# A routed expert layer's narrow last tiles: second product with the weights stationary, turned back at the end of the unit

## The chip, the core and the metric

The kernel runs on one core of one Trainium2 chip. The metric is the device time of one execution in microseconds (us); lower is better. Before the change three runs took 534.16, 530.08 and 535.13 us, median 534.16.

## What is computed

A block-sparse attention (4 batches, 8 heads, 768 positions, head size 64) gives 3072 tokens of 512 numbers. These go through a mixture of 8 experts: every token is sent to the one expert with the largest gate logit and multiplied by that token's two gates.

```
x = attention(q, k, v, sampled_blocks)          # [3072, 512]
e_idx = argmax(x @ w_gate)                       # one expert of 8 for each token
for e in range(8):
    mask = e_idx == e
    h  = maximum(x[mask] @ w1[e], 0)             # 512 -> 1024, first product
    ye = h @ w2[e]                               # 1024 -> 512, second product
    out[mask] = gate_w[mask] * eom[mask, e] * ye
```

Only the second product `h @ w2[e]` of some tokens, and the way to the output of those tokens, is touched by the change.

## The kernel before

**Stages.** The attention takes the first half of the span. From about 262 us on the kernel works through the experts in units. A unit is one expert's weights and up to three tiles of tokens. `SHAPE` (line 50) lists the tiles of each unit by their number of tokens: unit 0 to unit 13 run here, and the eight units behind them (`rest`, line 1302) stand under a branch on the number of tokens and are not entered in this input. Six of the fourteen units end in a tile of less than 128 tokens: unit 2 is [128, 128, 96], unit 4 [128, 128, 32], unit 10 [32], unit 11 [128, 64], unit 12 [128, 32], unit 13 [32]. All others are [128, 128].

**Steps.** Each unit has eight chunks of 128 hidden numbers (`NFC`), so there are 112 chunks, and one step of the program handles one chunk number n. `program` (line 1191) puts the functions of a step in order of a rank, and the engines carry them out in that order: the order on every engine is fixed (`in_order`). In step n stand: `w_h` and `w_l` of chunk n+6 (ScalarE and VectorE split the 32-bit weights into two 16-bit halves), `p_h` of chunk n (TensorE, first product, line 991), `p_y` of chunk n-4 (TensorE, second product, line 1031, since `YL` is 4), then `h_h` and `h_l` (ScalarE and VectorE split the hidden numbers into two 16-bit halves `hh`, `hl`). A unit u ends with its last `p_y` in step 8u+11. In step 8u+12 `y_o` (line 1059) scales the result by the gate on ScalarE and moves it from PSUM to SBUF, and a step later `store_y` (line 1067) writes the rows to their places with an indirect DMA of GpSimd.

**First product.** `p_h` keeps the weights stationary, 128x128 at a time, and moves the unit's tokens past them: 12 matmuls a chunk, as many columns as the unit has tokens.

**Second product.** `p_y` keeps the hidden numbers of a tile of t tokens stationary (128 by t) and moves 512 columns of w2 past them: three matmuls a chunk for a tile of 128 or 96 (hh with both halves of the weights, hl with one). For a tile of 32 or 64 tokens it cuts the 512 columns into 4 or 2 parts and writes them to different partitions of PSUM, so that each matmul uses 32 or 64 columns of the array: 12 matmuls of 128 columns, or 6 of 256. The result then lies as [128, 128] or [128, 256], and the table of output rows is made to fit this by three extra GpSimd instructions in `keep_t` (lines 880 to 886, with the constant `cb` of line 303).

**Buffers around it.** The hidden numbers come from two PSUM banks (`psT`, tag T). The results y stand in `psS` for units of more than one tile (the third tile, and the only tile of a unit of one, in `psO`, which has two banks). Converted weights go round a ring of 12 places, so `w_h` of chunk n waits for `p_y` of chunk n-12.

Of the kernel before, what the change touches and what calls it, by code (L numbers as in the profile page):

```python
# [9 lines left out]
F32 = mybir.dt.float32  # L10
F16 = mybir.dt.float16
I32 = mybir.dt.int32
AF = mybir.ActivationFunctionType
ALU = mybir.AluOpType
# [6 lines left out]
DM = H * D  # L21
E, FF = 8, 1024
NTOK = B * S
# [5 lines left out]
XP = DM + 16  # L29
# [20 lines left out]
SHAPE = [[128, 128]] + [widths(CAPS[w - NPU] if NPU <= w < NPU + NR else 8) for w in WALK]  # L50
# [10 lines left out]
YL = 4  # L61
# [65 lines left out]
def tile_kernel(ctx, tc, q, k, v, sampled, wg, wcat, out):  # L127
    nc = tc.nc
# [37 lines left out]
    ea = const.tile([128, 4], F32, name="ea")  # L166
    eai = const.tile([1, 1], I32, name="eai")
    xs0 = const.tile([128, 1024], F32, name="xs0")
    cb = const.tile([128, 2], F32, name="cb")
    rowid = const.tile([128, PS, MT], F32, name="rowid")  # L170
    arow = const.tile([128, 2], F32, name="arow")
    place_u = const.tile([128, 1 + PS, MT], I32, name="place_u")
# [119 lines left out]
    def setup_index():  # L292
        pp = psO.tile([128, 512], F32, tag="O", name="pp")
        for m in range(5):
            nc.tensor.matmul(pp[0:PS, m:m + 1], pw[:, :, m], ones[0:1, 0:1], start=True, stop=True)
        nc.vector.tensor_copy(index, pp[0:PS, 0:5])

        vf = sp.tile([128, 2, 12], F32, name="vf")
        nc.vector.tensor_copy(vf, vi)
        nc.vector.tensor_single_scalar(pb[:, 2:3], pb[:, 0:1], 63, op=ALU.bitwise_and)  # L300
        nc.vector.tensor_single_scalar(pb[:, 0:1], pb[:, 0:1], 6, op=ALU.arith_shift_right)
        nc.vector.tensor_single_scalar(pb[:, 1:2], pb[:, 1:2], 5, op=ALU.arith_shift_right)
        nc.vector.tensor_copy(cb, pb[:, 0:2])
        nc.vector.tensor_single_scalar(pb[:, 1:2], pb[:, 1:2], 1, op=ALU.bitwise_and)
        pf = sp.tile([128, 4], F32, name="pf")
        nc.vector.tensor_copy(pf[:, 0:2], pb[:, 0:2])
        nc.vector.tensor_copy(pf[:, 3:4], pb[:, 2:3])
        for w in range(NPU, NPU + NR):
            sh = widths(CAPS[w - NPU])
            if sh[-1] in (32, 64):  # L310
                m = len(sh) - 1
                nc.vector.tensor_single_scalar(
                    rowid[:, w, m:m + 1], rf if sh[-1] == 32 else pf[:, 3:4], 128.0 * m, op=ALU.add)

        nc.vector.scalar_tensor_tensor(pf[:, 2:3], pf[:, 0:1], 768.0, rf, op0=ALU.mult, op1=ALU.add)
        nc.vector.scalar_tensor_tensor(pf[:, 3:4], pf[:, 1:2], 736.0, pf[:, 2:3], op0=ALU.mult, op1=ALU.add)
        nc.vector.scalar_tensor_tensor(pf[:, 2:3], pf[:, 1:2], 32.0, pf[:, 2:3], op0=ALU.mult, op1=ALU.add)
        nc.vector.tensor_scalar(vf[:, :, 1:12], vf[:, :, 1:12], pf[:, 2:3], -32.0, op0=ALU.add, op1=ALU.add)
        nc.vector.tensor_scalar(vf[:, :, 0:1], vf[:, :, 0:1], pf[:, 3:4], None, op0=ALU.add)
        nc.vector.tensor_copy(vals, vf.rearrange("p a b -> p (a b)"))  # L320
# [532 lines left out]
    def piece(s, j):  # L853
        return rbuf[(8 * s + j) % NRAW]

    regs, tabs, xfs, xgs, xs, ws, hps, hs, ys, yos = {}, {}, {}, {}, {}, {}, {}, {}, {}, {}
    NP = NUNIT * NFC
    toks = [sum(sh) for sh in SHAPE]
    per = [2 if t <= 256 else 1 for t in toks]
# [8 lines left out]
    def keep_t(u):  # L868
        sh = SHAPE[u]
        m = len(sh)  # L870
        tab = rt.tile([128, MT], I32, tag="tab", name=f"tab{u}", bufs=4)
        gate = rt.tile([128, MT], F32, tag="gate", name=f"gate{u}", bufs=4)
        tabs[u] = tab, gate
        if not u:
            for n, x in enumerate(xfs[u]):
                nc.gpsimd.tensor_copy(gate[:, n:n + 1], x[:, DM + 1:DM + 2])
                nc.gpsimd.tensor_copy(tab[:, n:n + 1], x[:, DM:DM + 1])
            return
        nc.gpsimd.tensor_copy(gate[:, 0:m], xfs[u][:, :, DM + 1])
        if sh[-1] in (32, 64):  # L880
            m -= 1
            f = rt.tile([128, 1], F32, tag="tabf", name=f"tabf{u}")
            nc.gpsimd.tensor_single_scalar(f, xfs[u][:, m, DM:DM + 1], 128.0 / sh[-1], op=ALU.mult)
            c = 1 if sh[-1] == 32 else 0
            nc.gpsimd.tensor_tensor(f, f, cb[:, c:c + 1], op=ALU.add)
            nc.gpsimd.tensor_copy(tab[:, m:m + 1], f)
        if m:
            nc.gpsimd.tensor_copy(tab[:, 0:m], xfs[u][:, 0:m, DM])

    def load_w(n):  # L890
        if n in (0, 2, 8):
# [139 lines left out]
    def p_y(n):  # L1031
        u = n // 8
        hh, hl = hs[bank_of(n)]
        sh = SHAPE[u]
        if n % 8 == 0:
            y = ys[u] = []
            if u and len(sh) > 1:
                t = psS.tile([128, 2, 512], F32, tag="S", name=f"y{u}")
                y.extend((t[:, 0], t[:, 1]))
            while len(y) < len(sh):  # L1040
                y.append(psO.tile([128, 512], F32, tag="O", name=f"y{u}_{len(y)}"))
        k = cols(n).start
        if not u:
            for m in range(2):
                nc.tensor.matmul(  # L1045
                    ys[0][m], hh[:, k + 128 * m:k + 128 * m + 128], piece(0, n)[:, 512:1024], start=n == 0, stop=n == 7)
            return
        w = ws.pop(n)
        for t, y in zip(sh, ys[u]):
            parts = 128 // t if t in (32, 64) else 1  # L1050
            d = DM // parts
            for cnt, (a, l) in enumerate(((hh, 0), (hh, 1), (hl, 0))):
                for p in range(parts):
                    nc.tensor.matmul(  # L1054
                        y[t * p:t * p + t, 0:d], a[:, k:k + t], w[:, l, 512 + d * p:512 + d * p + d],
                        start=n % 8 == 0 and cnt == 0, stop=n % 8 == 7 and cnt == 2)
            k += t

    def y_o(u):
        yos[u] = []  # L1060
        for m, (w, y) in enumerate(zip(SHAPE[u], ys.pop(u))):
            rows_, d = (128, DM * w // 128) if w in (32, 64) else (w, DM)
            t = att.tile([128, XP], F32, tag="P", name=f"yo{u}_{m}", bufs=6)[0:rows_, 0:d]
            nc.scalar.activation(t, y[0:rows_, 0:d], AF.Copy, scale=tabs[u][1][0:rows_, m:m + 1])  # L1064
            yos[u].append(t)

    def store_y(u):
        tab = tabs.pop(u)[0]
        for m, (w, t) in enumerate(zip(SHAPE[u], yos.pop(u))):
            rows_, d = t.shape  # L1070
            c = DM // d
            i = nc.gpsimd.indirect_dma_start(  # L1072
                out.rearrange("n (c d) -> (n c) d", c=c), bass.IndirectOffsetOnAxis(ap=tab[0:rows_, m:m + 1], axis=0), t, None,
                bounds_check=NTOK * c - 1, oob_is_err=False).ins

            tc.declare_no_dep(i, group="out", reason="rows of out differ")
            tc.add_to_no_dep_group("out", i)
# [113 lines left out]
    def program(n0, n1):  # L1191
# [11 lines left out]
        for u in range(NUNIT):  # L1203
# [4 lines left out]
                do(max(t - 8, WW), 13, x_s, u)  # L1208
            do(max(t - 6, WW if u else 0), 13, keep_t, u)
            do(XT.get(u, max(t - 6, WW)), 15, x_t, u)  # L1210
            do(t + 8 + YL, 12, y_o, u)
            do(t + 8 + YL + 1, 13, store_y, u)
        for n in range(NP):
            w = max(n - LEAD, WW + (n - 8) // 2)
# [156 lines left out]
```

## Time and profile before

| | |
|---|---|
| runs | 534.16, 530.08, 535.13 us (median 534.16) |
| profiled execution, its time | 531.68 us |
| its span, first to last instruction | 529.9 us |
| TensorE clock granted, mean of the span | 0.982 of full |
| TensorE (PE) busy | 499.7 us, 94% |
| VectorE (DVE) busy | 358.4 us, 68% |
| ScalarE (ACT) busy | 305.8 us, 58% |
| GpSimd (POOL) busy | 256.8 us, 48% |

The span is cut by the profile into groups of instructions by the line that wrote them: L1007 is the first product, L1054 the second product of the units from 1 on, L1064 the scaling `y_o`, L1072 the store, L975 `w_h`, L979 `w_l`, L1021 `h_h`, L1029 `h_l`. The operands are named out<-in; a form 128\*32 128x128 is a stationary operand of 128 by 32 and a moving operand of 128 partitions by 128 columns. Matmuls are pipelined: the time from one start to the next is what a matmul takes from the engine, not the length of its own row. In the chain of waits the pieces follow each other without holes, so a piece's length there is such a distance.

### The profile page before, as it was taken

To read this page: it belongs to the slowest core of one execution; us is meant where nothing else is said; L and a number is where in the kernel's file an instruction comes from. 1 tells how busy PE (TensorE), PEld (TensorE's weight loads), DVE (VectorE), ACT (ScalarE), POOL (GpSimd) and SP (SyncE) were. 2 spreads that over 40 slices of the span, in tenths; PEclk is the share of its full clock that TensorE was granted. 3 is DMA by queue.
4 is the path that set the end of the run, shared out by engine and by line. 5 is a ranking of instruction groups with operands and counts; after the bars stand their busy time and mean duration, and the time that the engine had idled before them with its cause. 6 is when DMAs were issued, how large, how long until landed. Compare 5 with 4: busy or idle time off the path is not lost.

```text
span 529.9 us, 18428 instructions
## 1 busy us (share of the span) xinstructions
PE 499.7 (94%) x7403; PEld 348.9 (66%) x7403; DVE 358.4 (68%) x732; ACT 305.8 (58%) x542; POOL 256.8 (48%) x415
## 2 busy tenths in 40 slices
PE   7989998998988999989999999999999999998994
PEld 6756776766666777768556556666666666666663
DVE  2878879666787697857386545656566666578770
ACT  3646666575554665652376545655556656568661
POOL 7787778680576888854505130422404204126222
PEclk9999999899998999999999999999999999997998
DMA  7967888692976777768899999997998889899901
GB/s 299 300 223 220 259 260 298 216 312 89 274 226 188 240 218 240 243 231 306 295 387 330 409 275 331 354 249 243 260 274 314 250 240 328 233 273 335 220 30 36
DMA packets 63167, 136.60 MB, mean 258 GB/s; under 512 B 30560, under 2 KB 30688, under 8 KB 63074
## 3 DMA queue, kind: packets, MB, share of 16 engines
q1 hardware_dynamic: 50578, 91.56, 56.2%
q0 software_dynamic: 12496, 43.79, 24.7%
q8 instruction: 60, 0.98, 0.8%
q14 instruction: 33, 0.27, 0.1%
HBM read 116.25 MB, written 12.85 MB: 244 GB/s over the span
## 4 chain that ended last, share of the span: by engine, by line
PE 60%; POOL 14%; issue 12%; POOLq 5%; DMA 4%; DVE 4%; ACT 1%; ACTq 0%; DVEq 0%
PE h L1007 23%; PE y L1054 23%; POOL kr L436 7%; POOLq L425 4%; DMA vt<-in_v_dram,vidx 2%; PE S L504 2%; PE T L468 2%; PE h L1000 2%; PE y L1045 2%; POOL rows L757 2%; PE O L547 2%; POOL vt L453 1%; PE O L536 1%; DMA xb<-rows,place_u 1%; DVE mx L511 1%
## 5 line engine op out<-in xcount | busy, mean ns | idle before, releaser
L979 DVE SCALAR_TENSOR_TENSOR kr<-r,kr 128x1024 f16<-128x1024 f32 x77 | 93.8, 1224 | 59.4 <-ACT kr L975 59.0
L1072 POOL DMA_INDIRECT out_dram<-yo,tab x28 | 35.2, 1258 | 178.3 <-ACT yo L1064 174.1
L1007 PE MATMUL h<-xall,kr 128*128 128x256 f16 (+5 forms) x924 | 105.4, 264 | 2.3 <-DVE hh L1029 2.3
L1054 PE MATMUL y<-kr,hh 128*128 128x512 f16 (+3 forms) x675 | 104.3, 316 | 0.0
L975 ACT ACTIVATE kr<-r 128x1024 f16<-128x1024 f32 x77 | 80.8, 1055 | 39.7 <-PE y L1054 34.1
L1007 PEld LDWEIGHTS <-kr 128*128 128x128 f16 x924 | 80.2, 99 | 29.2 <-issue 6.0
L1054 PEld LDWEIGHTS <-hh 128*128 128x128 f16 (+3 forms) x936 | 56.8, 99 | 52.1 <-issue 11.1
L436 POOL TENSOR_TENSOR kr<-kn,eighth 128x256 f32<-128x256 f32 x132 | 79.7, 632 | 7.4 <-issue 5.5
L519 ACT ACTIVATE P<-S,mx 128x256 f32<-128x256 f32 x176 | 69.5, 488 | 9.4 <-DVE mx L511 9.2
L511 DVE TENSOR_REDUCE mx<-S 128x4 f32<-128x1024 f32 x44 | 53.6, 1219 | 21.4 <-ACT P L519 11.5
L453 POOL DMA_INDIRECT vt<-in_v_dram,vidx x44 | 44.4, 1010 | 29.2 <-PE O L547 18.6
L471 ACT COPY pt<-T 128x512 f32<-128x512 f32 x66 | 36.8, 592 | 29.2 <-PE T L468 29.2
L504 PE MATMUL S<-kr,qall 64*32 64x256 f32 x1408 | 50.5, 386 | 2.6 <-POOL kr L436 2.0
L468 PE MATMUL T<-ident,P 128*128 128x128 f32 x352 | 49.1, 284 | 0.0
L1021 ACT ACTIVATE hh<-h 128x512 f16<-128x512 f32 (+5 forms) x60 | 29.0, 484 | 32.2 <-PE y L1054 17.8
L979 DVE SCALAR_TENSOR_TENSOR ws<-r,ws 128x1024 f16<-128x1024 f32 x27 | 33.0, 1223 | 19.0 <-ACT ws L975 18.9
L1029 DVE SCALAR_TENSOR_TENSOR hh<-h,hh 128x512 f16<-128x512 f32 (+5 forms) x60 | 32.8, 546 | 15.3 <-ACT hh L1021 15.3
L468 PEld LDWEIGHTS T<-ident,P 128*128 128x128 f32 x352 | 40.3, 145 | 2.6 <-ACT P L519 0.3
L975 ACT ACTIVATE ws<-r 128x1024 f16<-128x1024 f32 x27 | 28.5, 1057 | 21.5 <-PE y L1054 18.1
L757 POOL DMA_INDIRECT rows<-xall,place x24 | 24.3, 1014 | 27.4 <-DVE dend L480 13.0
L536 PE MATMUL O<-vcall,pt 128*64 128x65 f32 x704 | 31.6, 227 | 5.9 <-DVE pt L473 2.0
L547 PE MATMUL O<-vt,pt 128*32 128x65 f32 x1408 | 31.5, 224 | 4.7 <-DMA vt<-in_v_dram,vidx 4.7
(277 smaller groups left out, 717.4 us busy)
## 6 DMA issues: line engine op xcount, KB each, us to landing
r<-in_wcat_dram SPq DMA_DIRECT2D x112, 512.0 KB, 5.4
vq<-in_v_dram SPq DMA_DIRECT2D x8, 780.0 KB, 5.0
qall<-in_q_dram SPq DMA_DIRECT2D x24, 256.0 KB, 4.5
vcall<-in_v_dram SPq DMA_DIRECT2D x22, 260.0 KB, 4.0
kn<-in_k_dram SPq DMA_DIRECT2D x10, 384.0 KB, 5.4
kn<-in_k_dram SPq DMA_DIRECT2D x3, 768.0 KB, 9.7
vcall<-in_v_dram SPq DMA_DIRECT2D x12, 130.0 KB, 9.4
vt<-in_v_dram,vidx POOLq DMA_INDIRECT x44, 5.3
```

What stands on the lines that cost most here:

```text
L436: nc.gpsimd.tensor_tensor(r[:, slot], kn[bp][:, :, ds(rv, 1)].rearrange("p u o n -> p u (o n)"), e8th, op=ALU.mult)
L453: nc.gpsimd.indirect_dma_start(vt[bp, i][:, s].rearrange("p b j w -> p (b j w)"), None, v, bass.IndirectOffsetOnAxis(ap=vidx[:, bp, i, s:s ...
L468: nc.tensor.transpose(pt[:, 128 * c:128 * c + 128], p[:, 128 * c:128 * c + 128], ident)
L504: nc.tensor.matmul(s[64 * b + 32 * qi:64 * b + 32 * qi + 32, h2, hp], t[p, 64 * j + 32 * qi:64 * j + 32 * qi + 32], g[p, 1 - qi:3:1 + qi, ...
L511: nc.vector.tensor_reduce(mx, self.s.rearrange("p b h n -> p (b h) n"), axis=AX.X, op=ALU.max, negate=True)
L519: nc.scalar.activation(p[:, 256 * hp:256 * hp + 256], self.s[:, b, hp], AF.Exp, bias=self.mx[:, 2 * b + hp:2 * b + hp + 1])
L536: nc.tensor.matmul(o[64 * b:64 * b + 64, h2, hp, 0:VW], t[:, col:col + 64], cv[:, h2, 4 * b + 2 * hg + hp], start=h2 == 0 and hp == 0, sto ...
L547: nc.tensor.matmul(o[row:row + 32, h2, hp, 0:VW], t[:, col:col + 32], av[:, qi, h2, j], start=False, stop=h2 == 1 and hp == 1)
L975: nc.scalar.activation(w[:, 0, r], piece(n // 8, n % 8)[:, r], AF.Copy, scale=SW)
L979: nc.vector.scalar_tensor_tensor(w[:, 1, r], piece(n // 8, n % 8)[:, r], SW, w[:, 0, r], op0=ALU.mult, op1=ALU.subtract)
L1007: nc.tensor.matmul(hps[g][:, cols(n)], w[:, hl, 128 * c:128 * c + 128], x[:, xl, c, 0:t], start=cnt == 0, stop=cnt == 11)
L1054: nc.tensor.matmul(y[t * p:t * p + t, 0:d], a[:, k:k + t], w[:, l, 512 + d * p:512 + d * p + d], start=n % 8 == 0 and cnt == 0, stop=n % 8 ...
```

## The change

For every tile under 128 tokens (so also the one of 96) `p_y` swaps the operands: a 128x128 piece of w2 is stationary, and the t tokens of hh or hl are the moving columns. The result stands turned, as four blocks [128, t] side by side in one PSUM bank, from 12 matmuls of t columns a chunk. At the end of the unit a new `y_c` copies these 4t columns to SBUF on ScalarE, a new `y_t` turns them back with four 32-bit transposes on TensorE into a new PSUM bank, and `y_o` then takes the tile as [t, 512]. The extra instructions in `keep_t` fall away, and the store writes t rows of 512 numbers. In step 8u+12 `y_c` has rank 5.5 (ahead of `w_h`), `y_t` rank 8.4 (behind `p_h`, ahead of `p_y`), `y_o` rank 11.5.

```diff
-        nc.vector.tensor_copy(cb, pb[:, 0:2])
...
         nc.gpsimd.tensor_copy(gate[:, 0:m], xfs[u][:, :, DM + 1])
-        if sh[-1] in (32, 64):
-            m -= 1
-            f = rt.tile([128, 1], F32, tag="tabf", name=f"tabf{u}")
-            nc.gpsimd.tensor_single_scalar(f, xfs[u][:, m, DM:DM + 1], 128.0 / sh[-1], op=ALU.mult)
-            c = 1 if sh[-1] == 32 else 0
-            nc.gpsimd.tensor_tensor(f, f, cb[:, c:c + 1], op=ALU.add)
-            nc.gpsimd.tensor_copy(tab[:, m:m + 1], f)
-        if m:
-            nc.gpsimd.tensor_copy(tab[:, 0:m], xfs[u][:, 0:m, DM])
+        nc.gpsimd.tensor_copy(tab[:, 0:m], xfs[u][:, :, DM])
...
         for t, y in zip(sh, ys[u]):
-            parts = 128 // t if t in (32, 64) else 1
-            d = DM // parts
+            if t < 128:
+                cnt = 0
+                for d in range(4):
+                    for a, l in ((hh, 0), (hl, 0), (hh, 1)):
+                        nc.tensor.matmul(
+                            y[:, t * d:t * d + t], w[:, l, 512 + 128 * d:640 + 128 * d], a[:, k:k + t],
+                            start=n % 8 == 0 and cnt == 0, stop=n % 8 == 7 and cnt == 11)
+                        cnt += 1
+                continue
             for cnt, (a, l) in enumerate(((hh, 0), (hh, 1), (hl, 0))):
-                for p in range(parts):
-                    nc.tensor.matmul(
-                        y[t * p:t * p + t, 0:d], a[:, k:k + t], w[:, l, 512 + d * p:512 + d * p + d],
-                        start=n % 8 == 0 and cnt == 0, stop=n % 8 == 7 and cnt == 2)
+                nc.tensor.matmul(
+                    y, a[:, k:k + t], w[:, l, 512:1024], start=n % 8 == 0 and cnt == 0, stop=n % 8 == 7 and cnt == 2)
             k += t
+
+    def y_c(u):
+        t = SHAPE[u][-1]
+        if t < 128:
+            y = ys[u].pop()
+            c = yts[u] = att.tile([128, XP], F32, tag="P", name=f"yt{u}", bufs=6)[:, 0:4 * t]
+            nc.scalar.copy(c, y[:, 0:4 * t])
+
+    def y_t(u):
+        t = SHAPE[u][-1]
+        if t < 128:
+            c = yts.pop(u)
+            y = psO.tile([128, 512], F32, tag="O", name=f"yr{u}")
+            for d in range(4):
+                nc.tensor.transpose(y[0:t, 128 * d:128 * d + 128], c[:, t * d:t * d + t], ident)
+            ys[u].append(y)
 
     def y_o(u):
...
-            rows_, d = (128, DM * w // 128) if w in (32, 64) else (w, DM)
-            t = att.tile([128, XP], F32, tag="P", name=f"yo{u}_{m}", bufs=6)[0:rows_, 0:d]
-            nc.scalar.activation(t, y[0:rows_, 0:d], AF.Copy, scale=tabs[u][1][0:rows_, m:m + 1])
+            t = att.tile([128, XP], F32, tag="P", name=f"yo{u}_{m}", bufs=6)[0:w, 0:DM]
+            nc.scalar.activation(t, y[0:w], AF.Copy, scale=tabs[u][1][0:w, m:m + 1])
...
             i = nc.gpsimd.indirect_dma_start(
-                out.rearrange("n (c d) -> (n c) d", c=c), bass.IndirectOffsetOnAxis(ap=tab[0:rows_, m:m + 1], axis=0), t, None,
-                bounds_check=NTOK * c - 1, oob_is_err=False).ins
+                out, bass.IndirectOffsetOnAxis(ap=tab[0:w, m:m + 1], axis=0), t, None,
+                bounds_check=NTOK - 1, oob_is_err=False).ins
...
-            do(t + 8 + YL, 12, y_o, u)
+            do(t + 8 + YL, 5.5, y_c, u)
+            do(t + 8 + YL, 8.4, y_t, u)
+            do(t + 8 + YL, 11.5, y_o, u)
```

## Rows read from the trace of the kernel before

**Rows 1.** The page: its chain by line, and two of its costliest groups.

```profile
PE h L1007 23%; PE y L1054 23%; POOL kr L436 7%; POOLq L425 4%; DMA vt<-in_v_dram,vidx 2%; PE S L504 2%; PE T L468 2%; PE h L1000 2%; PE y L1045 2%; POOL rows L757 2%; PE O L547 2%; POOL vt L453 1%; PE O L536 1%; DMA xb<-rows,place_u 1%; DVE mx L511 1%
L979 DVE SCALAR_TENSOR_TENSOR kr<-r,kr 128x1024 f16<-128x1024 f32 x77 | 93.8, 1224 | 59.4 <-ACT kr L975 59.0
...
L975 ACT ACTIVATE kr<-r 128x1024 f16<-128x1024 f32 x77 | 80.8, 1055 | 39.7 <-PE y L1054 34.1
```

**Rows 2.** Chain of waits, 255 to 530 us (start us, us, what): units 1, 2, 4.

```profile
262.25 0.66 PE xgp L951 x4
...
304.96 1.79 PE h L1007 x12
306.75 1.94 PE y L1054 x9
...
364.42 1.42 PE h L1007 x12
365.83 1.58 PE y L1054 x18
...
379.10 1.31 PE h L1007 x12
```

**Rows 3.** The same chain, later: units 9 to 12.

```profile
470.57 1.30 PE y L1054 x6
472.16 1.30 PE y L1054 x6
...
491.82 1.10 PE h L1007 x12
492.92 1.10 PE y L1054 x9
...
507.47 0.93 PE y L1054 x15
508.39 0.94 PE h L1007 x12
```

**Rows 4.** Timeline of PE, 470 to 530 us (start us, us, instructions, idle before).

```profile
477.16 0.47 PE L1007 MATMUL h<-xall,ws 128*128 128x32 f16 x12
...
477.84 0.47 PE L1007 MATMUL h<-xall,ws 128*128 128x32 f16 x12
...
481.54 2.08 PE L1007 MATMUL h<-xall,kr 128*128 128x192 f16 x12 [2.27 <-DVE hh L1029]
483.54 0.51 PE L1054 MATMUL y<-ws,hh 128*32 128x128 f16 x12
483.99 2.10 PE L1007 MATMUL h<-xall,kr 128*128 128x192 f16 x12
...
521.87 0.70 PE L1054 MATMUL y<-ws,hh 128*32 128x128 f16 x36
522.40 0.34 PE L1054 MATMUL y<-kr,hh 128*32 128x128 f16 x12
```

**Rows 5.** Stretches: busy us of PE, PEld, DVE, ACT, POOL (instructions), granted clock, DMA.

```profile
481.50:487.20 5.70, 5.67 (x53) 4.46 (x53) 5.70 (x6) 4.54 (x7) 5.46 (x6) 0.50 1.01 399
```

**Rows 6.** Timeline of PE, 199 to 203 us: eight 32-bit transposes.

```profile
199.75 1.09 PE L468 MATMUL T<-ident,P 128*128 128x128 f32 x8
```

**Rows 7.** Groups by line and shape on ACT: busy us, mean ns, idle before.

```profile
L1064 ACT ACTIVATE yo<-y,gate 128x512 f32<-128x512 f32 x22 | 14.1, 685 | 7.0 <-PE y L1054 5.6 <-issue 1.2 <-PE y L1045 0.2
...
L471 ACT COPY pt0d<-T0d 128x384 f32<-128x384 f32 x8 | 3.9, 484 | 0.4 <-PE T0d L468 0.4
```

**Rows 8.** Timeline of ACT: `h_h` in unit 11, the last scaling.

```profile
489.39 0.49 ACT L1021 ACTIVATE hh<-h 128x384 f16<-128x384 f32 x1
...
522.84 0.37 ACT L1064 ACTIVATE yo<-y,gate 128x128 f32<-128x128 f32 x1 [0.82 <-PE y L1054]
```

**Rows 9.** Timeline of DVE and of POOL: `h_l` in unit 11, the last store.

```profile
490.54 0.55 DVE L1029 SCALAR_TENSOR_TENSOR hh<-h,hh 128x384 f16<-128x384 f32 x1
...
523.99 0.97 POOL L1072 DMA_INDIRECT out_dram<-yo,tab  x1 [1.34 <-ACT yo L1064]
```

More of the change, by code (lines that the diff above doesn't have):

```diff
@@ L168, in tile_kernel @@
     xs0 = const.tile([128, 1024], F32, name="xs0")
-    cb = const.tile([128, 2], F32, name="cb")
     rowid = const.tile([128, PS, MT], F32, name="rowid")
@@ L854, in piece @@
         return rbuf[(8 * s + j) % NRAW]
-    regs, tabs, xfs, xgs, xs, ws, hps, hs, ys, yos = {}, {}, {}, {}, {}, {}, {}, {}, {}, {}
+    regs, tabs, xfs, xgs, xs, ws, hps, hs, ys, yos, yts = {}, {}, {}, {}, {}, {}, {}, {}, {}, {}, {}
     NP = NUNIT * NFC
@@ L1069, in store_y @@
         for m, (w, t) in enumerate(zip(SHAPE[u], yos.pop(u))):
-            rows_, d = t.shape
-            c = DM // d
             i = nc.gpsimd.indirect_dma_start(
-                out.rearrange("n (c d) -> (n c) d", c=c), bass.IndirectOffsetOnAxis(ap=tab[0:rows_, m:m + 1], axis=0), t, None,
-                bounds_check=NTOK * c - 1, oob_is_err=False).ins
+                out, bass.IndirectOffsetOnAxis(ap=tab[0:w, m:m + 1], axis=0), t, None,
+                bounds_check=NTOK - 1, oob_is_err=False).ins
             tc.declare_no_dep(i, group="out", reason="rows of out differ")
```

## The prediction

> **What bounds the kernel now.** First the page's chain by line, to see which engine the end hangs on: the two products, L1007 and L1054, hold 23% each, the most of any line, while ScalarE waits 34 us ahead of `w_h` for TensorE and VectorE 59 us ahead of `w_l` for ScalarE [rows 1]. Then the chain in order of time from 255 us on: it runs from h to y to h with no other engine between, so in the expert stage a matmul removed is time removed [rows 2, 3]. Then the timeline of TensorE, for the holes in that chain. There is one that matters: it stands 2.27 us ahead of unit 11's first h at 481.54, waiting for VectorE, and then works 5.7 us at half clock [rows 4, 5]. TensorE's time saved just ahead of that hole is only waited longer in it.
>
> **Price of one matmul.** From one piece to the next, 12 matmuls take 1.79 us at 352 columns and 1.31 at 256 [rows 2], which is 0.417 ns a column and 2.5 ns besides. So 12 of 192, 160, 96 and 64 columns are 0.99, 0.83, 0.51 and 0.35 us. A 512-wide one is 1.30/6 = 0.217 us, and 12 of 32 columns with 128x128 weights take 472.16 - 470.57 - 1.30 = 0.29, call it 0.30 [rows 3]; that is 25 ns each, more than the line gives (16), so a floor. The new second product has this same form (128x128 16-bit weights, narrow moving operand), so these prices hold for it.
>
> **What the tiled form costs.** Alone, the old 12 matmuls of 32 by 128 take (522.40 - 521.87)/3 = 0.177 us [rows 4], less than the new 0.30. Between full-width work they take more: in unit 4, h and y together are 3.00 us, of which h is 1.31 and the two full tiles 1.30, so 0.39 is left [rows 2, 3]. Some 0.2 us a step is lost in passing from one form of the array to the other and back. So the rows speak for the new form between wide work and against it alone.
> The Trainium skill (TensorEngine Tiling (Array Packing), Theoretical Speedup) gives tiles of 32 columns up to four times the rate and so speaks against the change. By that alone the 32-wide groups would lose 0.12 a step instead of gaining 0.09, in 28 steps 5.9 us, and the sum below would be +6.5 instead of +0.6. The same page (Key Properties) also says that a change of tiling mode drains the engine; the 0.2 us are this trace's number for it.
>
> **Second product, unit by unit** (eight chunks each):
> - Unit 2 (96): 9 x 0.217 = 1.94 [rows 2] becomes 6 x 0.217 + 0.51 = 1.81; gain 0.13 x 8 = 1.0 us.
> - Unit 4 (32): 0.39 becomes 0.30; gain 0.7.
> - Unit 10 (32): the first four chunks go from 0.68 a step (477.16 to 477.84) to 2 x 0.30, but stand ahead of the hole: 0. The last four lie behind it, two of them at half clock. There one y takes 0.45 [rows 4] besides what it adds to h; the new one lies between 0.30 (the floor stays) and 0.60 (everything doubles). I take 0.32, 32 columns at half pace, since the floor is above the column time. Gain 0.15 twice and 0.1 twice: 0.5.
> - Unit 11 (64): h and y 1.10 + 1.10 = 2.20 [rows 3], less 0.99 and 0.65 leaves 0.56; it becomes 0.35; gain 0.21 x 8 = 1.7.
> - Unit 12 (32): 0.93 + 0.94 = 1.87 [rows 3], less 0.83 and 0.65 leaves 0.39; becomes 0.30; gain 0.7.
> - Unit 13 (32): four steps of 0.68 become 0.60, gain 0.3; the last four have no h between, 0.177 becomes 0.30, loss 0.5. Together -0.2.
>
> Sum of gains 4.4 us.
>
> **Turning back, in the middle.** Five units end with others behind them. Their four transposes go on TensorE's path. Eight 128x128 ones are busy for 1.09 us with the last one's run-out in it [rows 6], so four are 0.5 us at most; I take 0.44, and for the four units whose transposed piece is 32 or 64 wide another 0.2 for the passage to a narrow form of the array and back, by the same measure as above: 0.44 + 4 x 0.64 = 3.0 us. Bounds: no passage, 2.2; each transpose waiting for the last, 0.66 a set of four plus 0.2 [rows 2], 4.3.
> `y_t` also waits for `y_c`. Cover is the h of that step, 1.31, 1.31, 0.99, 0.83 us and, in front of unit 13, only 0.30. `y_c` needs 0.1 after the last y (TensorE's row ends at 522.74, ScalarE begins at 522.84 [rows 4, 8]), some 0.2 of y's own pipeline, the copy (0.37 for 128 columns, 0.48 for 384 [rows 7, 8]) and 0.1 back: 0.77 to 0.9. It is hidden except before unit 13, where 0.46 us show. If the cover is gone everywhere (ScalarE late by one `w_h`), it is 1.06 us a unit.
>
> **ScalarE's queue.** `y_c` waits for TensorE, and behind it stand `w_h` and `h_h` of that step, which used to run ahead. Worst placed is unit 10's end: from the last y on, 0.66 for `y_c`, 1.06 `w_h`, 0.49 `h_h`, while VectorE does `w_l` (1.22) before `h_l` (0.55) [rows 1, 8, 9]: 0.66 + 1.06 + 1.22 + 0.55 = 3.5 us. The bank that `h_l` frees is wanted two steps on, after two h, two y and the transposes: 4.5 us. 1.0 us of slack, so nothing; the others have 0.7 to 2. The wider `y_o` (0.69 for 0.37) is hidden by ScalarE's waits for TensorE, 34 us in all [rows 1]; uncovered it would be 0.3 a unit.
>
> **The tail.** Behind unit 13's last y nothing covers anything: 0.1 + 0.37 for `y_c`, 0.1 to TensorE, four transposes from standstill 0.66 [rows 2], and `y_o` 0.69 for 0.37 [rows 7, 8]. 1.55 us.
>
> **At nothing.** GpSimd's three instructions in five units, and one small VectorE copy at the start: GpSimd waits for `y_o` before its stores, so nothing waits for the removed work. The stores of 32 rows of 2 KB for 128 of 512 B: the trace has no such store; the last one takes 0.97 [rows 9]. It could fall by all of that, or the longer rows could cost as much; I take 0, nearest to the row, and only the last store counts. The queues of SyncE are not touched.
>
> **Sum.** -4.4 + 3.0 + 0.46 + 1.55 = +0.6 us against the profiled 531.68: 532.3. That execution lies 2.5 below the median of the three runs, which spread over 5 us. I set the number on the middle of all four (531.68 and 534.16, so 532.9): 533.5 us.
>
> **The rivals.**
> - *The forecast* (the terms as above): -2.5 to +3 about the sum, within 1%. Chance 0.76.
> - *Slower: tiling was worth its name.* The 0.2 a step that I put to the passage between array forms belongs to the second product itself (its wait behind h, its write to PSUM), and stays with the new form, on top of 0.30. Decides if a new narrow group takes 0.5 between wide ones instead of 0.30. 32 steps are on the path (8 + 4 + 8 + 8 + 4): +6.4, so 532.9 + 7.0 = 539.9. For it: alone, the tiled form is the faster, 0.177 to 0.30. Against: h of the same form next to the 512-wide y shows no such loss [rows 3]. Chance 0.06. The tiling page of the Trainium skill, read alone (above), leads here.
> - *Slower: TensorE stands at `y_t`.* ScalarE comes to `y_c` one `w_h` late at four units: +4.2, 537.7. Against: it waits for TensorE ahead of its work [rows 1]. Chance 0.07.
> - *No gain behind the hole.* The units 10 to 12 are held by weight conversion, VectorE's 1.22 + 0.55/2 = 1.5 us a chunk. Then 2.9 of the gains go: 536.4. Against: the chain from 487 us on holds nothing but TensorE [rows 3]. Chance 0.05.
> - *Faster: the hole without its half clock.* TensorE works 5.7 us at half clock behind 2.27 us of standing [rows 4, 5], and 2.85 come back if the clock stays up: 530.6. The new form keeps the whole array in use ahead of it, but is also done 0.3 sooner, so the standing grows. Chance 0.06.
>
> **How the numbers follow.** The forecast's own range is 530.4 to 536.5; the runs' spread of 2.5 to either side and the rivals at 536 to 540 stretch it to 529.5 to 538. Faster by over 1% (about what a measurement of this kernel can tell from no change) would need 5.3 us: the whole 4.4 with nothing paid back, or the clock and free transposes together: 0.05. Slower by over 1%: the first slower rival, and the second at its upper end: 0.07. Within 1%: 0.88.
>
> **What would show it.** In the trace after: unit 4's h and y together about 2.91 instead of 3.00, unit 11's 1.99 instead of 2.20; the pieces of unit 13's last steps 0.30 apart; four transposes a unit, starting 0.11 apart, with no idle time in front of them but before unit 13; the last `y_o` some 1.5 us further behind the last y. The prediction fails if idle time stands before the transposes in other units, if the new narrow groups take more than 0.4 us, or if the clock falls elsewhere.

## The result: 0.9% slower, where no change was forecast

| | before | after |
|---|---|---|
| median of 22 runs each | 531.87 us | 537.90 us |
| lowest and highest | 527.97, 539.52 | 531.79, 545.45 |
| ratio, 95% interval | | 1.0092 [1.0063, 1.0122] |
| profiled execution, its span | 531.68, 529.9 us | 539.58, 537.8 us |

The prediction was 533.5 us, with 0.88 on "within 1%". The time is at the upper end of its range (538.0), and the interval excludes no change. The ratio leaves out every run more than 1.5% above the fastest of its kernel, and is smaller than the quotient of the medians (1.0113).

**Where the time went.** The first product of each unit (`h`) is a mark that both programs have. In the two profiled executions unit 2 begins 0.23 us later after the change than before; its fifth chunk 0.45 later; unit 3 begins 5.54 later, its fifth chunk 7.40 later, unit 4 7.83 later; the end is 7.88 later. So from unit 4 on, where the prediction expected most of its plus and minus, the sum is +0.05 us, and all of the difference between these two lies in one place ahead of unit 3 and just behind it.

The timeline of TensorE of the changed kernel there (start us, us, engine, line, what; in brackets the idle time before and what ended it):

```profile
315.38 0.67 PE L1044 MATMUL y<-hh,kr 128*128 128x96 f16 x12
322.81 2.72 PE L997 MATMUL h<-xall,ws 128*128 128x256 f16 x12 [6.75 <-DMA xall<-vcall]
325.32 2.65 PE L1050 MATMUL y<-kr,hh 128*128 128x512 f16 x6
327.81 0.67 PE L1044 MATMUL y<-hh,kr 128*128 128x96 f16 x12
328.32 1.48 PE L997 MATMUL h<-xall,ws 128*128 128x256 f16 x12
```

TensorE stands 6.75 us for `xall`, the turned tokens of unit 3, and then takes 2.51 us from h to y where 1.31 is usual [rows 2]. The busy times and the granted clock by stretch (us, busy and count of five engines, PEclk, DMA share, GB/s) say why:

```profile
302.00:316.00 14.00, 14.00 (x118) 8.76 (x116) 7.00 (x8) 6.50 (x10) 5.35 (x6) 1.00 1.12 293
316.00:322.80 6.80, 0.06 (x2) 0.03 (x1) 3.42 (x3) 2.78 (x3) 0.00 (x0) 0.86 1.09 143
322.80:327.80 5.00, 5.00 (x18) 2.61 (x19) 0.00 (x0) 0.00 (x0) 0.00 (x0) 0.51 1.02 405
327.80:348.00 20.20, 20.20 (x177) 14.61 (x176) 9.77 (x10) 11.30 (x16) 6.14 (x6) 1.00 0.93 268
```

Behind the stand the granted clock is 0.51, the 1.2 GHz level, for 5 us; then 1.00 again. The same place in the kernel before, in its timeline: a stand of 1.10 us and no half clock behind it (1.47 for the h, as usual). Below it, its chain of waits there, and its DMA view from 307.5 to 312 us (median us from issue to landing).

```profile
317.26 1.47 PE L1007 MATMUL h<-xall,ws 128*128 128x256 f16 x12 [1.10 <-DVE hh L1029]
...
316.69 0.53 DVE hh L1029
317.22 0.04 issue
317.26 1.47 PE h L1007 x12
...
xall<-vcall SPq DMA_TRANSPOSE x1, 9.9
```

The row and the chain name VectorE, whose instruction ended just before. But the second of unit 3's two transposing DMAs (`x_t`, below) was issued at 307.26 and landed 9.87 us later, at 317.12, which is 0.14 ahead of the h, as 322.67 is ahead of 322.81 in the changed kernel. So this stand, too, ended with that transfer.

So 0.45 that it was late already, +5.65 for the stand, +2.4 for the clock, less 0.14 in each of eight chunks of the new second product, four on either side of the stand: that is the +7.4. The chain of waits of the changed kernel names the transfer (start us, us, what):

```profile
308.36 0.52 PE y L1044 x12
308.88 0.79 SPq L932
309.67 0.04 issue
309.71 12.96 DMA xall<-vcall
322.67 0.14 issue
322.81 2.72 PE h L997 x12
```

L932 is `x_t`, the DMA on SyncE that turns a unit's tokens (128 tokens of 1024 16-bit numbers, 256 KB each). Unit 3 has two. The second takes 12.96 us from its issue to its landing.

**The prediction's own places**, in TensorE's timeline of the changed kernel: unit 4, the hole ahead of unit 11, unit 10 behind it and its transposes, unit 11, unit 13 and the tail.

```profile
371.85 1.47 PE L997 MATMUL h<-xall,kr 128*128 128x256 f16 x12
...
374.45 0.45 PE L1044 MATMUL y<-hh,ws 128*128 128x32 f16 x12
374.75 1.47 PE L997 MATMUL h<-xall,kr 128*128 128x256 f16 x12
...
489.11 2.08 PE L997 MATMUL h<-xall,kr 128*128 128x192 f16 x12 [2.48 <-DVE hh L1019]
490.98 0.53 PE L1044 MATMUL y<-hh,ws 128*128 128x32 f16 x12
491.35 2.08 PE L997 MATMUL h<-xall,kr 128*128 128x192 f16 x12
...
497.82 0.60 PE L1067 MATMUL yr<-ident,yt 128*32 128x128 f32 x4
498.25 0.81 PE L1050 MATMUL y<-kr,hh 128*128 128x512 f16 x3
...
503.23 1.16 PE L997 MATMUL h<-xall,kr 128*128 128x192 f16 x12
...
504.86 0.51 PE L1044 MATMUL y<-hh,kr 128*128 128x64 f16 x12
505.21 0.99 PE L997 MATMUL h<-xall,ws 128*128 128x160 f16 x12
...
525.07 0.45 PE L997 MATMUL h<-xall,ws 128*128 128x32 f16 x12
525.58 0.61 PE L1067 MATMUL yr<-ident,yt 128*32 128x128 f32 x4
...
528.14 1.05 PE L1044 MATMUL y<-hh,ws 128*128 128x32 f16 x36
529.04 0.45 PE L1044 MATMUL y<-hh,kr 128*128 128x32 f16 x12
529.84 0.61 PE L1067 MATMUL yr<-ident,yt 128*32 128x128 f32 x4 [0.35 <-ACT yt L1059]
```

Read from start to start: unit 4's h and y take 374.75 - 371.85 = 2.90 us, unit 11's 1.98, a set of four transposes 0.43, and unit 13's last three pieces 0.30 each. Only the last transposes have idle time noted in front. ScalarE at the end of the same run (its last copy and scaling, answering to [rows 8]):

```profile
529.52 0.27 ACT L1059 COPY yt<-y 128x128 f32<-128x128 f32 x1 [1.28 <-PE y L1044]
530.54 0.68 ACT L1074 ACTIVATE yo<-yr,gate 32x512 f32<-32x512 f32 x1 [0.75 <-PE yr L1067]
```

### The profile page after: what moved, and what is told of

It reads as the page before. It is cut to its first block, busy times and chain, and to the rows that moved or that the text cites. A ratio compares the mean times of both kernels' runs of the same rounds, so it can differ in the third digit from the quotient of the medians.

```text
span 537.8 us, 18712 instructions
## 1 busy us (share of the span) xinstructions
PE 501.8 (93%) x7547; PEld 361.3 (67%) x7547; DVE 358.3 (67%) x731; ACT 305.7 (57%) x548; POOL 252.1 (47%) x402
## 4 chain that ended last, share of the span: by engine, by line
PE 72%; DVE 8%; DMA 7%; POOL 4%; issue 4%; SPq 2%; ACT 1%; POOLq 1%; ACTq 0%; DVEq 0%
PE h L997 20%; PE y L1050 17%; PE T L466 6%; PE S L502 6%; PE O L545 4%; PE O L534 4%; DMA xall<-vcall 3%; PE h L990 3%; PE y L1044 3%; PE xp L625 2%; PE lp L641 2%; DVE mx L509 2%; DMA r<-in_wcat_dram 2%; PE y L1035 1%; PE warm L184 1%
## 5 line engine op out<-in xcount | busy, mean ns | idle before, releaser
L1050 PE MATMUL y<-kr,hh 128*128 128x512 f16 x363 | 90.5, 383 | 0.0
L1050 PEld LDWEIGHTS <-hh 128*128 128x128 f16 x480 | 46.4, 98 | 39.1 <-issue 1.1
L997 PE MATMUL h<-xall,ws 128*128 128x256 f16 (+3 forms) x324 | 33.9, 254 | 7.2 <-DMA xall<-vcall 6.7
L965 ACT ACTIVATE ws<-r 128x1024 f16<-128x1024 f32 x27 | 28.4, 1057 | 16.1 <-PE y L1050 11.5
```

The source lines that it names most:

```text
L965: nc.scalar.activation(w[:, 0, r], piece(n // 8, n % 8)[:, r], AF.Copy, scale=SW)
L997: nc.tensor.matmul(hps[g][:, cols(n)], w[:, hl, 128 * c:128 * c + 128], x[:, xl, c, 0:t], start=cnt == 0, stop=cnt == 11)
L1050: nc.tensor.matmul(y, a[:, k:k + t], w[:, l, 512:1024], start=n % 8 == 0 and cnt == 0, stop=n % 8 == 7 and cnt == 2)
```

## The experiments

Theory A: the loss is the stand ahead of unit 3; it comes from unit 3's transposing DMAs running at the same time as the gathers of unit 5's rows (`load_x(5)`, GpSimd, indirect DMAs), and what the prediction summed up is right beside it. Rivals: the new narrow second product itself costs what is lost; the placement of the buffers, which shifts with the removed constant `cb`, brings it; the removed constant's copy brings it; the transposing DMAs are slow at this place by themselves. The expectations use short names: layout for the placement, schedule and stall for the longer wait for unit 3's transposing DMAs, narrow-stretch and instruction for the cost of the new second product itself, theory B for what would stay with the gathers moved.

One table for all runs; ratios quoted below have their intervals there. "Stand" is the idle time ahead of unit 3's first h in the profiled execution; "2.0 to 3.4" is the time from unit 2's first h to the first h of unit 3's fifth chunk, so it holds the stand and what follows it; "4.0 to end" is from unit 4's first h to the end of the span. The profile is one execution; the ratio stands on the runs of each kernel, taken as in the result.

| kernel | stand | 2.0 to 3.4 | 4.0 to end | ratio to before, 95% |
|---|---|---|---|---|
| before | 1.10 | 41.54 | 189.21 | |
| after | 6.75 | 48.71 | 189.26 | 1.0092 [1.0063, 1.0122] |
| e11 after again | 3.04 | 44.05 | 189.12 | 1.0057 [1.0018, 1.0097] |
| e16 after again | 3.35 | 44.37 | 188.75 | 1.0041 [0.9999, 1.0082] |
| e1 after, buffers aligned | 5.76 | 48.07 | 190.82 | 1.0061 [1.0016, 1.0105] |
| e10 after, buffers as before | 4.71 | 47.62 | 189.01 | 1.0051 [1.0007, 1.0095] |
| e2 before, buffers 32 B off | 2.05 | 42.63 | 190.76 | 1.0013 [0.9973, 1.0053] |
| e9 before, buffers as after | 0.48 | 40.92 | 188.94 | 0.9981 [0.9937, 1.0025] |
| e15 all six turned, `cb` kept | 2.81 | 43.63 | 187.91 | 1.0059 [1.0018, 1.0099] |
| e3 after, unit 2 as before | 3.03 | 43.47 | 190.74 | 1.0102 [1.0065, 1.0138] |
| e4 unit 2 alone turned | 3.09 | 44.05 | 189.15 | 1.0000 [0.9961, 1.0039] |
| e5 without unit 13 | 2.09 | 43.10 | 188.46 | 0.9888 [0.9799, 0.9977] |
| e6 without units 10, 13 | 2.57 | 41.91 | 187.65 | 1.0023 [0.9985, 1.0062] |
| e7 after, turns earlier | none | 39.18 | 188.60 | 0.9965 [0.9924, 1.0007] |
| e8 before, turns earlier | none | 40.28 | 188.31 | 0.9952 [0.9912, 0.9992] |
| e13 after, gathers later | none | 39.46 | 196.58 | 1.0091 [1.0056, 1.0126] |
| e14 before, gathers later | none | 40.28 | 190.75 | 1.0001 [0.9965, 1.0038] |
| e17 after, gathers and split later | 0.92 | 40.26 | 188.87 | 0.9993 [0.9960, 1.0026] |
| e18 before, the same | none | 40.90 | 189.16 | 1.0020 [0.9989, 1.0051] |
| e12 units 2, 4, 11, 12, turns earlier | none | 39.18 | 187.66 | 0.9892 [0.9849, 0.9936] |

The runs were on several chips, and each ratio is to the kernel before on its own chip. e1 to e4 ran on a chip on which every kernel took 2% longer (last section).

**Placement: e1, e2, e9, e10.**

```diff
 # e1 (on after), e2 (on before): 8 bytes a partition that nobody uses
+    const.tile([128, 2], F32, name="pad")
 # e9 (on before): cb inside another constant, tabf in another pool
-    cb = const.tile([128, 2], F32, name="cb")
-    arow = const.tile([128, 2], F32, name="arow")
+    arow4 = const.tile([128, 4], F32, name="arow")
+    arow, cb = arow4[:, 0:2], arow4[:, 2:4]
 # e10 (on after): both of the removed tiles' places kept free
+    const.tile([128, 2], F32, name="pad")
+    rt.tile([128, 1], F32, tag="tabf", name="pad2")
```

> The changed kernel with one tile of 8 bytes a partition put back where cb stood, so that every large SBUF buffer starts again on a multiple of 64 bytes, as before the change (in the changed kernel all of them start 32 bytes off). Layout theory: most of the +0.92% is the layout, so this comes to +0.0 to +0.3% of the kernel before, and its trace shows no stand of 5 us or more ahead of unit 3. Schedule theory (the narrower second product of unit 2 moves the transposing DMAs of unit 3 into other traffic): stays at +0.6 to +1.2%. The sum of the prediction alone: +0.1%.

> The kernel before with one extra unused tile of 8 bytes a partition, so that its large SBUF buffers start 32 bytes off a multiple of 64; no instruction differs. Layout theory: slower by 0.5 to 1.1%. Schedule theory and the prediction's sum: 0.0%, within 0.3%.

> The kernel before with cb put into the spare half of arow's slot and tabf into another pool, so that every large buffer lies at the very address that it has in the changed kernel (weight pieces 32 bytes lower, the rings of kr, x and the gathered tokens 96 lower); no instruction is added or taken away. Layout theory (second form: it is the place of the rings, not the offset of 32, that lengthens the stand ahead of unit 3): +0.6 to +1.2%, a stand of 5 us or more ahead of unit 3. Instruction theory (the turned units themselves cost it): 0.0%, within 0.3%.

> The changed kernel with unused tiles in the places of cb and tabf, so that all large buffers lie where they lay before the change. Layout theory, second form: -0.2 to +0.2%, a stand of 3 us or less ahead of unit 3. Instruction theory: +0.6 to +1.1%.

Measured: the changed kernel stays slow with its buffers back at the old places (1.0061, 1.0051), and the old one stays as it was with the new places (1.0013, 0.9981). Together the four put placement out; e10 alone would not, since its interval reaches down to 1.0007.

**Which units: e3, e4, e5, e6.** e3 is the changed kernel with unit 2's tile of 96 as before (`if t < 96` for `t < 128`); the others are the kernel before with the new code for some units alone.

```diff
+TURN = (2, 4, 10, 11, 12)       # e5; e6: (2, 4, 11, 12); e4: `t == 96` in place of both conditions
-            if t < 128:
+            if t < 128 and u in TURN:
```

> The changed kernel with unit 2's tile of 96 tokens computed as before; the tiles of 32 and 64 stay turned, the buffers stay 32 bytes off. Schedule theory: the loss goes, to +0.0 to +0.3%. Layout theory: stays at +0.7 to +1.2%, with the stand ahead of unit 3. The prediction's sum alone: +0.2% (unit 2's gain of 1.0 us and its transposes of 0.44 go).

> The kernel before with only unit 2's tile of 96 turned; cb and the tables stay, so the buffers lie as before. Schedule theory: slower by 0.6 to 1.2%. Layout theory: the same or faster by 0.1% (1.0 us gained, 0.44 paid back).

> All narrow tiles turned but the last unit's (13), which stays tiled and is stored as before; buffers lie as before the change. Narrow-stretch theory (the loss is made where TensorE has nothing but 32-column matmuls, in units 10 and 13, and behind the last of them): the tail of about 2 us and the slower last steps go, so at most +0.3% against the kernel before. Stall theory (the loss is a longer stand ahead of unit 3, waiting for the transposing DMAs of its tokens): stays at +0.6 to +1.0%. The prediction's own sum without its tail and unit 13: -0.2%.

> Units 10 and 13 both left tiled, units 2, 4, 11 and 12 turned. Narrow-stretch theory: no loss left, -0.4 to +0.1%. Stall theory: stays at +0.6 to +1.0%. The prediction's own sum: -0.3%.

Measured: no single unit carries the loss. With unit 2 alone turned the time is that of before (1.0000), with all but unit 2 it is 1.0102, both against the schedule theory. Where e3's 1.0102 is lost its profile does not show: that execution is the fastest of its runs, 0.84 us behind e2's from 2.0 to 3.4 and level with it from 4.0 on. e6's 1.0023 lies under the 1.006 to 1.010 of the stall theory. e5's ratio rests on few runs: its six runs average 534.1 us to 535.2 of before, 4.5 either way, which says little. The last stretch says more: with units 10 and 13 left tiled it takes 187.65 us (e12, below, 187.66), under every kernel with all six turned (187.91 to 189.26 on the other chips, e13 left out; kernels with nothing turned lie as low as 188.31, so this is a small difference); with 13 alone left tiled 188.46.

**Moving the transposing DMAs: e7, e8.** `XT` holds the steps of `x_t`; unit 3's goes from step 18 to 16, ahead of the gathers.

```diff
-XT = {1: 6}
+XT = {1: 6, 3: 16}
```

> The changed kernel with unit 3's transposing DMAs issued two steps earlier (step 16 for 18). Stall theory: the stand ahead of unit 3 goes from the trace and this comes within 0.2% of its twin, the kernel before with the same edit. Narrow-stretch theory: whatever the edit does, this stays 0.6 to 1.0% slower than the twin.

> The kernel before with unit 3's transposing DMAs issued two steps earlier: the twin of the run above. Stall theory: its stand of about 1 us ahead of unit 3 goes, 0.0 to -0.5% against the kernel before. Narrow-stretch theory: the same, and the other twin 0.6 to 1.0% above it.

TensorE's timeline of the changed kernel with this edit: unit 3's h follows unit 2's y with no idle time, at full clock.

```profile
311.62 0.67 PE L1044 MATMUL y<-hh,kr 128*128 128x96 f16 x12
312.13 1.47 PE L997 MATMUL h<-xall,ws 128*128 128x256 f16 x12
```

Both kernels gain, and the changed one is no longer behind: 530.64 to 532.36 us, means of 12 runs each, 1.7 us in its favour (1.9 either way); by the ratios the two are alike. The rival that the narrow second product costs the time falls with this: it would have left the changed kernel behind.

**Moving the gathers: e13, e14, then e17, e18.** The transposing DMAs stay; unit 5's gathers go from step 24 to 30, behind unit 2's stores in GpSimd's queue. e17 and e18 also move the splitting of these rows (`x_s`) and their transposing DMAs to step 35.

```diff
-                do(max(t - 16, PLAN[2]), 6, load_x, u)
+                do(30 if u == 5 else max(t - 16, PLAN[2]), 6, load_x, u)
 # e17, e18 also
-                do(max(t - 8, WW), 13, x_s, u)
+                do(35 if u == 5 else max(t - 8, WW), 13, x_s, u)
-            do(XT.get(u, max(t - 6, WW)), 15, x_t, u)
+            do(35 if u == 5 else XT.get(u, max(t - 6, WW)), 15, x_t, u)
```

> The changed kernel with one thing moved: the gathers of unit 5's rows (three descriptors' worth of GpSimd work in step 24) go behind unit 2's stores (step 30), so that they no longer run at the same time as unit 3's two transposing DMAs; these stay where they are. Theory A (the stand ahead of unit 3 is the gathers and the transposing DMAs slowing each other): the stand falls under 1 us, the transposing DMA instructions take about 1.3 us each instead of 4 to 7, u2.4 to u3.4 comes to 28 us or less from 31.7 to 36.2, and the time falls by 2 to 6 us below the unaltered changed kernel of this call. Theory B (the transposing DMAs are slow by themselves at this place, because of the weight loads): the stand stays 2 to 6 us and the time is the unaltered one's within 1.5 us. New collisions are possible at step 30, with unit 4's second product under way; then a loss of 1 to 2 us shows after unit 3.

> The kernel before with the same move of unit 5's gathers. Theory A: its shorter stand (0.5 to 1.1 us) goes too and it gains 1 to 2.5 us on the kernel before, and lies 0 to 2 us above the changed kernel with the same move, as the pair with the earlier transposing DMAs did. Theory B: no gain, ratio 1.000 within 0.003.

The stand ahead of unit 3 goes in both (2.0 to 3.4: 39.46 and 40.28 us, as with the earlier transposing DMAs). How the transfers run in the 24 us from 300 on is to be seen in the DMA view of this stretch (queues: packets, MB, share of 16 engines; issues: KB each, median us from issue to landing). The changed kernel:

```profile
q0 software_dynamic: 320, 1.07, 25.1%
...
xall<-vcall SPq DMA_TRANSPOSE x2, 13.0
...
xb<-rows,place_u POOLq DMA_INDIRECT x2, 12.6
```

The changed kernel without the gathers there (e13):

```profile
q0 software_dynamic: 160, 0.52, 5.4%
...
r<-in_wcat_dram SPq DMA_DIRECT2D x9, 512.0 KB, 5.1
xall<-vcall SPq DMA_TRANSPOSE x4, 6.8
```

The changed kernel with the earlier transposing DMAs and the gathers in their place (e7):

```profile
q0 software_dynamic: 320, 1.07, 10.9%
```

And in e13's timelines of SyncE and TensorE, the second transposing DMA of unit 3 and unit 3's first h:

```profile
307.72 3.71 SPq L932 DMA_TRANSPOSE xall<-vcall  x1
...
315.10 1.47 PE L997 MATMUL h<-xall,ws 128*128 128x256 f16 x12
```

The software queue's 160 packets in e13, those of unit 1's stores, took 0.054 x 16 x 24 / 160 = 0.13 us each. The changed kernel has 160 more there, those of the gathers; if its stores took the same, the gathers' packets took (0.251 - 0.054) x 16 x 24 / 160 = 0.47 us each, by this estimate. Without it: the same 320 packets of stores and gathers took 0.251 x 16 x 24 / 320 = 0.30 us each in the changed kernel and 0.109 x 16 x 24 / 320 = 0.13 in e7. The other way round, unit 3's second transposing DMA landed after 13.0 us in the changed kernel; in e13 its landing is not in the trace (the 6.8 is that of one of unit 4's), but unit 3's h starts 315.10 - 307.72 = 7.4 us after its issue and does not stand. Each slows the other: that is the collision. It is there before the change too (9.9 us), and the kernel before with late gathers (e14) shows what it takes: 41.54 becomes 40.28. One expectation for e13 missed: the two transposing instructions were to take about 1.3 us each and held SyncE for 9.91 us together, against 11.25 in the changed kernel, so most of that time is not the gathers'.

But the time of e13 is no better (1.0091): the late rows hold up ScalarE, which comes to `x_s(5)` ahead of unit 4's `hh`. ScalarE's timeline in e13:

```profile
344.46 1.06 ACT L919 ACTIVATE vcall<-xb 128x1024 f16<-128x1024 f32 x1 [6.55 <-DMA xb<-rows,place_u]
```

And TensorE's timeline in e13:

```profile
348.33 3.04 PE L997 MATMUL h<-xall,kr 128*128 128x288 f16 x12 [4.23 <-DVE hh L1019]
351.16 2.77 PE L1050 MATMUL y<-kr,hh 128*128 128x512 f16 x6
```

A new stand of 4.23 us with half clock behind it (3.04 for 1.63): one wait was exchanged for another, by my edit. e14's time gained nothing either (1.0001, where 1 to 2.5 us were expected): its stretch from 4.0 to the end is 1.5 us longer than before. So the splitting was moved as well:

> The changed kernel with unit 5's gathers behind unit 2's stores (step 30), and with the splitting of unit 5's tokens and their transposing DMAs in step 35, so that ScalarE and VectorE do not wait for the late gathers ahead of unit 4's h_h and h_l. In the first kernel with late gathers they did: 4.2 us of TensorE standing and 7.3 us in all, ahead of unit 4's third h. Theory A (gathers and unit 3's transposing DMAs slow each other, and that is the whole loss): no stand ahead of unit 3, none in unit 4, time 2.5 to 7 us under the unaltered changed kernel's usual place (1.006 of before), so a ratio of 0.993 to 1.000 to the kernel before. Theory B (something else holds the changed kernel back by the same amount wherever the gathers stand): ratio 1.003 or more.

> The kernel before with the same two moves. Theory A: no stand ahead of unit 3, ratio 0.994 to 0.999, and 0 to 1 us above or below the changed kernel with the same moves (the earlier pair with early transposing DMAs had 1.7 us between the means). Theory B: as the kernel before, 1.000, and 2 us or more below the changed kernel.

TensorE's timeline of e17: 0.92 us ahead of unit 3, no half clock, nothing in unit 4.

```profile
314.82 1.47 PE L997 MATMUL h<-xall,ws 128*128 128x256 f16 x12 [0.92 <-DMA xall<-vcall]
```

The changed kernel is at 0.9993 [0.9960, 1.0026] instead of 1.004 to 1.009, and 1.9 us (1.85 either way) under its twin e18 by the means of 12 runs each, 531.06 and 533.00. With the collision out of the way, by either edit, the loss is gone. That part of theory A is shown. That the transposing DMAs are slow by themselves is out as the cause of the loss, though not as a part of their time. e18 itself gained nothing measurable, against the expectation of 0.994 to 0.999.

**The constant, and the kernel again: e11, e15, e16.** e11 and e16 have no edit. e15 is the kernel before with `TURN` holding all six units, so that `cb` and its copy on VectorE stay.

> The changed kernel unaltered, on this chip beside the others. Both theories: +0.6 to +1.2%, a stand of 5 us or more ahead of unit 3. If it is within 0.3% here, the loss goes with the chip and neither theory is told apart.

> The kernel before with all six narrow tiles turned, exactly as the change turns them, but with the unused constant of the old output table and its copy on VectorE left in, so that the buffers lie where they lay before. If the loss is that of turning (the stand ahead of unit 3 grows, the tiled units 10 and 13 give 1.3 us away): ratio to before 1.004 to 1.009, and within 1.5 us of the unaltered changed kernel of this call. If the loss came with the removed constant (its copy or the placement that follows): ratio 0.998 to 1.002, 2.5 us or more below the changed kernel.

> The changed kernel unaltered, as the twin of the other three on this chip. Ratio to before 1.005 to 1.010 as in the runs so far; a stand of 3 to 7 us ahead of unit 3's first product.

Measured: e15 loses as the changed kernel does on the same chip (1.0059 to 1.0041), so the removed constant has nothing to do with it. The repeats show how much one profile says: the same program stood 6.75, 3.04 and 3.35 us. Their rows in TensorE's timeline, e11:

```profile
318.54 2.27 PE L997 MATMUL h<-xall,ws 128*128 128x256 f16 x12 [3.04 <-DMA xall<-vcall]
```

and e16:

```profile
317.43 2.55 PE L997 MATMUL h<-xall,ws 128*128 128x256 f16 x12 [3.35 <-DMA xall<-vcall]
```

**The best version: e12.** Units 2, 4, 11 and 12 turned, 10 and 13 tiled, unit 3's transposing DMAs in step 16.

> Units 2, 4, 11 and 12 turned, 10 and 13 left tiled, unit 3's transposing DMAs two steps earlier, buffers as before the change. By the stand alone -0.5% (its twin without turning gave that), and the four turned units another 1.5 us by the traces so far: -0.7 to -1.0%. If turning has a cost of its own that the early transposes do not cure, 0.0%.

Measured: 528.94 us, 527.89 to 530.06 in six runs; ratio 0.9892 [0.9849, 0.9936]. It beats both kernels. Its runs spread over 2.2 us, the changed kernel's over 13.7; but these are six runs, and e7's twelve, with the same earlier transposing DMAs, spread over 9.7, so a smaller spread is not shown.

**What stays open.** Why the transposing DMAs and the gathers collide for longer in the changed kernel, when the work issued up to that place is nearly the same. All profiles of kernels with nothing turned show a stand of 0.48 to 2.05 us there, all with some unit turned and both transfers in place 2.09 to 6.75. By the landing of unit 3's second transposing DMA the collision is longer in the changed kernel (13.0, 10.5 in e11, 11.3 in e16, and 12.4 in e10, to 9.9 before), but not in e5 and e6 (9.1 and 9.5). Placement, the constant and the turned unit 2 taken alone are excluded. That TensorE comes to the wait sooner with unit 2 turned explains 0.55 us (four chunks by 0.14); it doesn't explain e3, whose unit 2 is as before. Open, too, is when the half clock follows: it did behind 2.09 us of stand in e5 and did not behind 2.57 in e6 or 3.03 in e3, so the length of the stand alone does not decide it.

## Why the prediction was wrong, by its steps

- **The step that failed: "There is one [hole] that matters".** It read TensorE's holes for the one at unit 11 [rows 4, 5] and took the stand of 1.10 us ahead of unit 3 for nothing. That stand was the visible end of a transfer that landed at 317.12, 0.14 ahead of the h; the row named VectorE, and the transfer did not appear in the chain (shown above; [rows 2] leaves this stretch out). The sum therefore had no term for TensorE arriving there sooner, nor for a transfer that lands later; "The queues of SyncE are not touched" was true of the program, and not of the time its transfers took. Measured in three profiles of the changed kernel: between +1.4 (e11's 29.92 us from unit 2's to unit 3's first h, to 28.54 before) and +5.3 us (33.85), and another 1.7 to 2.4 for the half clock behind it (14.13 in e11 and e16 and 14.86 from there to unit 3's fifth chunk, to 12.46 at full clock in e7). No rival held this. That 537.9 still lies within the range, and next to the 537.7 of "TensorE stands at `y_t`", is luck: what brings it there is in none of its terms. (The range's own lower end, 530.4, was taken 2.5 under 532.9; under the 533.5 that it was to surround it would have been 531.0.)
- **Price of a matmul: right.** 12 of 96 columns take 0.51, of 64 0.35, of 32 0.30 (forecast: the same). Unit 4 2.90 (2.91), unit 11 1.98 (1.99). The rival "tiling was worth its name" is out: new narrow groups take 0.30 between wide ones, not 0.50. The page TensorEngine Tiling (Array Packing) of the Trainium skill, section Theoretical Speedup, which spoke against the change, does not decide here.
- **Unit 2: right, but hidden.** Forecast 1.0 us; with the collision gone it is 40.28 - 39.18 = 1.1 (e8, e7). In the kernel as changed it is spent waiting.
- **Transposes: 0.43 a set as forecast, without the 0.2 for the passage.** Sets of 32 and 64 wide take the same 0.43 to 0.44 as those of 96: 0.8 us less than summed.
- **`y_t` before unit 13:** 525.58 - 525.07 - 0.30 = 0.2 instead of 0.46. Elsewhere no wait, so "TensorE stands at `y_t`" is out.
- **Unit 10:** nothing ahead of the hole (11.43 us from its first h to unit 11's, before and after), 0.37 at half clock (forecast 0.32). From unit 11's first to its fifth h it gains 0.3 (8.02 to 7.72), forecast 0.5. The hole and its half clock stayed, so "faster: the hole without its half clock" is out, and so is "no gain behind the hole".
- **The tail: 0.4 smaller.** From unit 13's fifth h to the end the change costs +2.07. Of this 0.66 are unit 12's transposes and the wait ahead of them, -0.2 the steps with an h, +0.48 the lone groups (forecast 0.5), and +1.13 what follows the last y (forecast 1.55). The copy took 0.27 instead of 0.37, the last `y_o` stood 0.95 further behind the last y (forecast 1.23) and was 0.31 longer.
- **Sum from unit 4 on:** forecast 0.6 + 1.0 - 0.44 = +1.2, measured +0.05; the difference is the passage that was not there (0.8), the shorter wait (0.25) and the shorter tail (0.4), less some 0.3 that units 10 and 13 gained less. Without the collision's growth the forecast would have been a little too high, by about 1 us.

## What to carry to other kernels

A small stand ahead of a stage may be a transfer with no slack even where the row names an engine: ask when the transfer landed, what it runs beside, and what its time is with that out of the way, before costing a change as a sum over one engine. In this kernel transposing DMAs and gathers are best kept apart in time; moving one of them two steps earlier gave the kernel before 2.8 us (e8, means, 1.6 either way), more than any part of the change. When the transfer is moved, its consumers in the in-order queues have to move too.

## What the runs showed of the hardware that was not expected

- Transposing DMAs and gathers slow each other: unit 3's second transposing DMA landed after 13.0 us (9.9 before the change) and within 7.4 with the gathers moved (e13); packets of stores and gathers took 0.30 us and 0.13 with the transposing DMAs moved (e7). Even without the gathers, 256 KB transposed (unit 4's) took 6.8, 5.1 and 6.5 us from issue to landing where 512 KB of weights took 5.1, 6.7 and 5.4 (e13, e14, e17): half the bytes in about the same time. The Trainium skill (Advanced Engine Details and Errata, X-Bar Transpose (TRN2)) calls transposing DMAs as fast as regular ones; this trace differs.
- Four 32-bit transposes with a stationary operand 32, 64 or 96 wide cost TensorE the same 0.43 to 0.44 us between 128-wide work, while the 32-wide 16-bit groups of the kernel before lost 0.2 a step there.
- On one chip (e1 to e4) TensorE stood where the profile shows nothing that it waited for: 10 to 12 us in the attention, 0.5 to 2.4 on the other chips, and in runs of 32-column matmuls about every 0.73 us. That it waited for its own instructions is a guess that no run here tests. TensorE's timeline in e3, the last chunks of unit 13:

```profile
531.39 0.29 PE L1044 MATMUL y<-hh,kr 128*128 128x32 f16 x5 [0.29 <-issue]
532.11 0.30 PE L1044 MATMUL y<-hh,kr 128*128 128x32 f16 x6 [0.43 <-issue]
532.84 1.18 PE L1044 MATMUL y<-hh,ws 128*128 128x32 f16 x36 [0.42 <-issue]
```

  In the expert stage the other chips have no such holes. They cost the kernels with more narrow matmuls more, 3.0 us there in e1 and e3 to 1.3 in e2 and 1.5 in e4, which is part of e1's and e3's ratio.
